# A convolution and expert kernel: the experts begin behind the first sort, and copies, first sums and the filter image are rearranged

## The chip, the core and the metric

The kernel runs on one core of a Trainium2 chip. The metric is the device time of one execution in microseconds (us); lower is better. Below, PE is the matrix engine (PEld its weight loads), DVE the vector engine, ACT the scalar engine, POOL the GpSimd engine and SP the engine that issues most of the DMAs. Each engine works through its own instructions in order.

## The reference

Eight sequences of 5696 rows of 128 columns are convolved with one filter along the rows. Each resulting row goes to one of eight two-layer expert networks, the one with the largest gate logit, and is scaled by its gate weight.

```python
L = 2 * S                                   # x: (8, 5696, 128), h: (5696, 128)
y = irfft(rfft(x, L, axis=1) * rfft(h, L, axis=0), L, axis=1)[:, :S]
x = y.reshape(B * S, D)                     # 45568 rows
logits = x @ w_gate                         # 8 experts
e = argmax(logits, axis=1)
gate_w = softmax(logits)[row, e]
out[row] = gate_w * (relu(x[row] @ w1[e]) @ w2[e])   # w1[e]: 128x1024, w2[e]: 1024x128
```

## The kernel before

The Fourier transforms are matrix products in two steps, and the eight sequences are worked on in three groups of 2, 3 and 3 (`SPLIT`). Names in the profile end in or contain the group's number in the order's rows (`pa1`, `xp1`, `mh1`), and the trace leaves the numbers out.

- **Transforms** (`phase_a`, `steps_a`): PE multiplies 120-row pieces of x (`xt`, split into `xc`) by a cosine and a sine matrix into `pa`; ACT and DVE copy the results (`ut`), and SP stores them in DRAM as `U`. The second and third group have 72 such steps each. The filter goes the same way once (`phase_h`, result `uht`).
- **Products** (`phase_b`), 120 items a group: SP loads `uq` from `U`; PE does the second step of the transform (`xp`); DVE multiplies by the filter's image `hh`, one product into `zt` and two halves into `xs` (L492, L495); POOL adds `zt` and `xs` (`combine`, L502: the first sums); PE transforms back (`vp`), and the result is copied to `vt` (`save`, L519: the result copies) and stored as `V`. The first group also makes the filter's image: PE multiplies (`hp`), ACT scales it into `hh` (L448), and SP stores it as `HS`, from which the two later groups load it.
- **Sort** (`phase_c`), 24 rounds of two steps (16 rounds in the first group): PE finishes the inverse transform (`yp`), ACT copies rows to `rt`, PE transposes and takes the logits (`tp`, `gb`), DVE finds each row's expert and place (`pi`), and POOL scatters the rows to the sorted table `SR` by indirect DMA (L581), 96 scatters in the first group and 144 in each later one. `pi` has 4 buffers. During the sort of the second group the transforms of the third are done as a guest. At the end `tables` (on DVE) lists the tiles of 256 rows.
- **Experts** (`moe`): for each tile SP loads rows `xr` from `SR` (7 buffers) and, when the expert changes, 2 MB of weights `wb` from `WD`; PE does layer 1 (`mh`, L985) and layer 2 (`ma`, L1005), ACT and DVE make the relu's two parts `hs` between them, DVE scales the result into `xr`, and POOL scatters it to `out` (L1028). Part 0, 1 and 2 of the tiles (37, 67 and 81) can begin when the first, second and third group is sorted. All scatters of a group must have landed before its first `xr` load.

The order of the instructions on every engine is fixed when the program is written: generators yield an estimated cost, and `run` takes the stream that is furthest behind, its cost divided by its share. `RATE` scales the costs of the background stream: entries 0, 1 and 2 are the second group's transforms, products and sort, 3, 4 and 5 the third group's. `LULL` is a pause of the expert stream behind the first sort, in which only the background stream runs, and its share there. After the third sort only experts are left.

```python
        run((first, 1.0), (prep, SHARES[1]), (back, SHARES[2]), until=first)
        run((prep, 1.0))
        lull = pause(LULL[0])
        run((lull, 1.0), (back, LULL[1]), until=lull)
        run((experts(), 1.0), (back, SHARES[3]))
```

Of the kernel before, what the change touches and what calls it, by code (L numbers as in the profile page):

```python
# [13 lines left out]
F32 = mybir.dt.float32  # L14
# [4 lines left out]
ALU = mybir.AluOpType  # L19
# [4 lines left out]
NB = 48  # L24
MB = 119
QN = 120
MP = 120
HP = 64
# [14 lines left out]
SAVEV = ()  # L43
# [5 lines left out]
GAPS = (0, 6000, 5000)  # L49
HOLD = (0, 0, 0)  # L50
AHEAD = 2
HEAD = 26000
A3 = (True, True, False)
ALO = ('gpsimd', 'vector', 'vector')
# [1 line left out]
WARM = 7  # L56
TURN = (1, 1, 1)
LOGIT = (2, 2, 2)
LULL = (29000, 0.448)
RARE = 3  # L60
XR = 7
RATE = (0.372, 0.559, 0.45, 0.8, 0.78, 0.6)


@with_exitstack
def conv_moe(ctx: ExitStack, tc: tile.TileContext, I, out, B, S, D, E, F, split):
    nc = tc.nc
# [67 lines left out]
    for g, nbs in enumerate(split):  # L135
# [7 lines left out]
            parts.append(gr.parts[-1])  # L143
            b0 += nb
        groups.append(gr)
    HS = dram.tile([P, QN, 2, D], F32, name="HS")
    WD = dram.tile([4, E * P, F], F32, name="WD")

    queue = []
# [158 lines left out]
    def phase_a(gr):  # L308
        start, begin, store, flush, M = steps_a(gr, "six", SIX)
        half = AT if gr.g == 0 else 750 * RATE[3 * gr.g - 3]  # L310
        start()
        for m in range(M + 2):
            if m < M:
                begin(m)
            yield half
            flush()
            if 1 <= m <= M:
                store(m - 1)
        yield 0
        flush()  # L320

    class Guest:
        def __init__(self, gr):
# [74 lines left out]
    def phase_b(gr):  # L398
# [15 lines left out]
        def load(qb):  # L414
            q = qb * QB
            if q >= QN:
                return
            uq = sb.tile([K2, QB, gr.cols], F32, tag="ld", name=f"uq{g}_{q}", bufs=LD if g else 3)
            nc.sync.dma_start(uq, gr.U[q : q + QB].rearrange("q p c -> p q c"))
            mi = mibufs[qb % 4]  # L420
            for k in range(2):
                nc.sync.dma_start(mi[k * HP : k * HP + NB], I["miq"][k * NB : (k + 1) * NB, q : q + QB, :])
            if g != 0:
                hhs[qb] = hhbufs[qb % 3]
                nc.sync.dma_start(hhs[qb][:, :QB], HS[:, q : q + QB])
            tiles[qb] = (uq, mi)

        mats, hhs, hbank, cuts = {}, {}, {}, {}
# [11 lines left out]
        def filt_save(qb, m):  # L440
            if qb not in hbank:
                return
            hp = hbank[qb]
            if m == 0:
                hhs[qb] = hhbufs[qb % 3]
            hh = hhs[qb]
            c2, k = divmod(m, 2)
            nc.scalar.mul(hh[k * HP : (k + 1) * HP, :, c2, :], hp[c2 * HP : (c2 + 1) * HP], -1.0 if m == 3 else 1.0)  # L448
            if m == 3:
                hbank.pop(qb)  # L450
                late.append((HS[:, qb * QB : qb * QB + QB], hh[:, :QB]))

        def forward(n):
            q, c = items[n]
# [44 lines left out]

        def combine(n):  # L500
            zt, xs = state[n]
            nc.gpsimd.tensor_tensor(out=zt, in0=zt, in1=xs, op=ALU.add)  # L502

        def inverse(n):
            q, c = items[n]
# [7 lines left out]
        def save(n):  # L513
            q, c = items[n]
            qb, k0 = divmod(q, QB)
            if k0 == 0 and c == 0:
                outs_[qb] = sb.tile([K2, QB, gr.cols], F32, tag="six", name=f"vt{g}_{q}", bufs=SIX)
            cp = nc.vector.tensor_copy if g == 0 or n % 4 in SAVEV else nc.scalar.copy
            cp(outs_[qb][:, k0, c * cw : (c + 1) * cw], banks.pop(n)[:K2, :cw])  # L519
            if k0 == QB - 1 and c == nch - 1:  # L520
                late.append((gr.V[qb * QB : qb * QB + QB].rearrange("q p c -> p q c"), outs_.pop(qb)))
                tiles.pop(qb), hhs.pop(qb), mats.pop(qb)
# [609 lines left out]
    def pause(ns):  # L1132
        yield ns
# [3 lines left out]
    def run(*streams, until=None, stop=()):  # L1137
        live = [[0.0, i, s, share] for i, (s, share) in enumerate(streams)]
        held = []
        while any(t[2] not in stop for t in live):  # L1140
            live.sort(key=lambda t: t[:2])
            it = live.pop(0)
            cost = next(it[2], DONE)
            if cost is None:
                held.append(it)
                continue
            now = it[0]
            if cost is DONE:
                if it[2] is until:
                    return  # L1150
            else:
                it[0] += cost / it[3]
                live.append(it)
            for t in held:
                t[0] = max(t[0], now)
            live += held
            held = []

    g0 = groups[0]
    with tc.manual_schedule():  # L1160
        prep = weights()
        back = rest()
        run((phase_a(g0), 1.0), (phase_h(), SHARES[4]), (consts(), 1.0), (prep, SHARES[5]), stop=(prep,))
        sb.close()
        sb.open("b")
        first = phase_b(g0)
        run((first, 1.0), (prep, SHARES[0]), until=first)
        sb.close()
        sb.close()
        sb.open("sb")  # L1170
        first = chain(*[gather(pt) for pt in g0.parts])
        run((first, 1.0), (prep, SHARES[1]), (back, SHARES[2]), until=first)
        run((prep, 1.0))
        lull = pause(LULL[0])
        run((lull, 1.0), (back, LULL[1]), until=lull)
        run((experts(), 1.0), (back, SHARES[3]))
        sb.close()
# [78 lines left out]
```

## Time and profile before

| | |
|---|---|
| time, median of 3 runs | 2405.68 us (2403.33 to 2406.07) |
| profiled execution: time, span | 2400.84 us, 2399.1 us |
| busy share of the span | PE 89%, DVE 67%, POOL 47%, ACT 44% |
| granted clock of PE, mean of the profiled execution | 0.951 of full speed |
| first group: products | about 117 to 340 us |
| first group: sort, with transforms of the second | about 366 to 495 us |
| first matmul of an expert | 570 us |
| first expert matmul of part 1 and end of the third sort on PE | 1190.5 us and about 1732 us |

The busy shares are means over stages with different limits. The stages' limits are read from the rows below: by stretch, a row of windows gives the busy time of every engine, PE's granted clock (1.00 is 2.4 GHz, 0.5 is 1.2 GHz) and the busy share of the DMA engines.

### The profile page before, as it was taken

How to read it: one execution, taken by the hardware profiler on the slowest of the kernel's cores; microseconds unless marked ns; L12 is line 12 of the kernel's file. 1: busy time of each engine (PE TensorE's matmuls, PEld its weight loads, DVE VectorE, ACT ScalarE, POOL GpSimd, SP SyncE). 2: the span in 40 equal slices, each digit the busy share in tenths (PEclk: the TensorE clock that was granted, in tenths of full speed). 3: DMA queues.
4: the chain of work that ended last, by engine and by line, in shares of the span. 5: the costliest groups of instructions: out<-in, count | busy, mean ns of one | idle time of the engine just before them, and what ended most of it. 6: DMA issues, size and time to landing. Idle time of an engine off the chain costs nothing.

```text
span 2399.1 us, 46517 instructions
## 1 busy us (share of the span) xinstructions
PE 2125.5 (89%) x13998; PEld 1759.0 (73%) x13998; DVE 1602.7 (67%) x3987; ACT 1049.3 (44%) x2233; POOL 1136.7 (47%) x1161
## 2 busy tenths in 40 slices
PE   7777759767999989998699998999979999999997
PEld 4654435444777777775377777988878999999997
DVE  3599965456999846667688885676654455555554
ACT  4533315432443445553144444665534444444443
POOL 5333323663555516677545553577762233333332
PEclk8899989878999999998799999999989999999998
DMA  9988879779999768877778775566322222222220
GB/s 268 294 256 266 271 205 321 234 214 265 271 269 276 213 191 248 258 234 218 220 202 252 210 236 148 124 167 175 95 87 85 76 74 81 75 79 75 80 75 30
DMA packets 226940, 444.88 MB, mean 185 GB/s; under 512 B 30993, under 2 KB 141639, under 8 KB 226688
## 3 DMA queue, kind: packets, MB, share of 16 engines
q1 hardware_dynamic: 202752, 394.78, 56.4%
q0 software_dynamic: 23936, 47.09, 6.5%
q8 instruction: 115, 1.88, 0.3%
q14 instruction: 137, 1.12, 0.2%
HBM read 597.98 MB, written 175.89 MB: 323 GB/s over the span
## 4 chain that ended last, share of the span: by engine, by line
PE 61%; DMA 12%; issue 6%; DVE 4%; POOL 2%; SPq 2%; ACT 1%; POOLq 0%; DVEq 0%; ACTq 0%
PE mh L985 18%; PE ma L1005 18%; PE vp L510 5%; PE xp L467 5%; DMA wb<-WD 5%; PE yp L644 5%; PE pa L279 3%; PE mx L167 2%; DMA SR<-rt,pi 2%; DMA xt<-x 2%; PE tp L683 1%; PE tp L167 1%; POOL out L1028 1%; DVE xs L495 1%; POOL SR L581 1%
## 5 line engine op out<-in xcount | busy, mean ns | idle before, releaser
L993 DVE SCALAR_TENSOR_TENSOR hs<-mh,hs 128x512 fp32r<-128x512 f32 x728 | 502.6, 691 | 473.4 <-ACT hs L991 467.6
L985 PE MATMUL mh<-xtb,wb 128*128 128x256 f32 x4368 | 728.8, 303 | 41.4 <-DMA wb<-WD 30.4
L985 PEld LDWEIGHTS mh<-xtb,wb 128*128 128x128 f32 x4368 | 596.6, 192 | 127.6 <-issue 66.2
L1028 POOL DMA_INDIRECT out<-xr x364 | 362.7, 996 | 681.1 <-DVE xr L1019 606.2
L1005 PE MATMUL ma<-hs,wb 128*128 128x256 f32 x4368 | 659.9, 287 | 10.4 <-DMA wb<-WD 10.2
L991 ACT ACTIVATE hs<-mh 128x512 fp32r<-128x512 f32 x728 | 435.3, 598 | 520.4 <-PE mh L985 518.3
L1005 PEld LDWEIGHTS ma<-hs,wb 128*128 128x128 f32 x4368 | 577.4, 192 | 14.4 <-DMA wb<-WD 13.9
L581 POOL DMA_INDIRECT SR<-rt,pi x384 | 397.3, 1035 | 208.5 <-issue 68.5
L502 POOL TENSOR_TENSOR zt<-zt,xs 128x384 f32<-128x384 f32 (+1 forms) x360 | 324.9, 916 | 313.2 <-DVE xs L495 303.5
L495 DVE TENSOR_TENSOR xs<-xp,hh 64x384 f32<-64x384 f32 (+1 forms) x720 | 367.8, 511 | 26.3 <-POOL zt L502 14.8
L467 PE MATMUL xp<-uq,mt 96*128 96x384 f32 (+1 forms) x720 | 284.1, 478 | 84.4 <-DVE xs L495 53.0
L510 PE MATMUL vp<-zt,mi 128*96 128x384 f32 (+1 forms) x720 | 269.9, 456 | 19.4 <-POOL zt L502 17.2
L519 ACT COPY vt<-vp 96x384 f32<-96x384 f32 x240 | 114.1, 475 | 358.3 <-PE vp L510 349.2
L467 PEld LDWEIGHTS xp<-uq,mt 96*128 96x128 f32 x720 | 118.8, 197 | 133.3 <-PE hp L438 60.9
L492 DVE TENSOR_TENSOR zt<-xp,hh 128x384 f32<-128x384 f32 (+1 forms) x360 | 183.3, 509 | 39.8 <-PE xp L467 19.5
L510 PEld LDWEIGHTS vp<-zt,mi 128*96 128x96 f32 x720 | 108.8, 164 | 113.4 <-issue 58.0
L279 PE MATMUL pa<-xc,fcr 120*120 120x512 f32 x360 | 110.6, 446 | 32.1 <-ACT xc L257 12.4
L448 ACT ACTIVATE hh<-hp 64x512 f32<-64x512 f32 x120 | 70.9, 591 | 142.4 <-issue 100.9
L644 PE MATMUL yp<-vr,gcr 120*120 120x384 f32 x576 | 117.0, 338 | 0.0
L632 DVE TENSOR_TENSOR vr<-vq,vr 120x768 fp32r<-120x768 f32 x96 | 91.5, 955 | 34.2 <-ACT vr L631 33.7
L279 PEld LDWEIGHTS pa<-xc,fcr 120*120 120x120 f32 x360 | 68.0, 203 | 59.0 <-ACT xc L257 17.2
L644 PEld LDWEIGHTS yp<-vr,gcr 120*120 120x120 f32 x576 | 96.2, 183 | 0.3 <-DVE vr L632 0.3
(121 smaller groups left out, 2028.3 us busy)
## 6 DMA issues: line engine op xcount, KB each, us to landing
wb<-WD SPq DMA_DIRECT2D x728, 512.0 KB
vq<-V SPq DMA_DIRECT2D x64, 720.0 KB
U<-ut SPq DMA_DIRECT2D x48, 720.0 KB
uq<-U SPq DMA_DIRECT2D x60, 576.0 KB
V<-vt SPq DMA_DIRECT2D x60, 576.0 KB
hh<-HS SPq DMA_DIRECT2D x60, 512.0 KB
xr<-SR SPq DMA_DIRECT2D x182, 130.0 KB
xt<-x SPq DMA_DIRECT2D x96, 240.0 KB
```

What stands on the lines that cost most here:

```text
L279: nc.tensor.matmul(banks[m][:QN, :], lhs, rhs, start=(k == 0), stop=(k == len(ops) - 1))
L467: nc.tensor.matmul(xp[:, :cw], mt[:, k0, :], uc, start=True, stop=True)
L495: nc.vector.tensor_tensor(out=xs[to], in0=x3[at], in1=hv[at, 1].broadcast_to([HP, cb, D]), op=ALU.mult)
L502: nc.gpsimd.tensor_tensor(out=zt, in0=zt, in1=xs, op=ALU.add)
L510: nc.tensor.matmul(vp[:K2, :cw], mi[:, k0, :], zt.rearrange("p b d -> p (b d)"), start=True, stop=True)
L581: s = nc.gpsimd.indirect_dma_start(out=SR[:, :], out_offset=IndirectOffsetOnAxis(ap=pi[:, b : b + 1], axis=0), in_=rt[:, b, :], in_offset= ...
L644: nc.tensor.matmul(yp[:MP, :cw], lhs, rhs, start=(m == 0), stop=(m == len(ops) - 1))
L985: nc.tensor.matmul(hp[:, u, :], wb[:, a, f, :], xt[:, b, :], start=(n == 0), stop=(n == 2))
L991: done = nc.scalar.activation(hs[:, 0], hp, AF.Relu)
L993: nc.vector.scalar_tensor_tensor(out=hs[:, 1], in0=hp, scalar=0.0, in1=hs[:, 0].bitcast(F32), op0=ALU.max, op1=ALU.subtract)
L1005: nc.tensor.matmul(accs[j], wb[:, a, f, :], hs[:, b, u, :], start=(k == 0 and u == 0 and n == 0), stop=(k == NPAIR - 1 and u == 1 and n == 2),
L1028: sc = nc.gpsimd.indirect_dma_start(out=out[:, :], out_offset=IndirectOffsetOnAxis(ap=xr[:, s, D + 1 : D + 2].bitcast(I32), axis=0), in_=x ...
```

## The change

Five things are edited. (1) All result copies go to ACT; before, those of the first group were on DVE. (2) `LULL` is shortened from 29000 to 12000, and from then on a step of the second group's transforms counts 1000 (`SLOW`) instead of 279, so that they are spread between the first expert tiles. (3) `RATE` gives the second group's products and sort lower costs (more of them per expert tile) and the third group's sort a higher cost (less of it per tile). (4) The first 20 sums of the third group are done by DVE (`ALONE`). (5) `HS` keeps 48 of every 64 partitions, in two DMAs instead of one for a store and for a load. No arithmetic is changed.

```diff
+ALONE = 20
-LULL = (29000, 0.448)
+LULL = (12000, 0.448)
+SLOW = 1000
-RATE = (0.372, 0.559, 0.45, 0.8, 0.78, 0.6)
+RATE = (0.372, 0.48, 0.42, 0.8, 0.78, 0.7)
...
-    HS = dram.tile([P, QN, 2, D], F32, name="HS")
+    HS = dram.tile([2, NB, QN, 2, D], F32, name="HS")
...
         for m in range(M + 2):
             if m < M:
                 begin(m)
-            yield half
+            yield half if not marks["experts"] else SLOW
             flush()
...
-                nc.sync.dma_start(hhs[qb][:, :QB], HS[:, q : q + QB])
+                for k in range(2):
+                    nc.sync.dma_start(hhs[qb][k * HP : k * HP + NB, :QB], HS[k, :, q : q + QB])
...
-                late.append((HS[:, qb * QB : qb * QB + QB], hh[:, :QB]))
+                for k2 in range(2):
+                    late.append((HS[k2, :, qb * QB : qb * QB + QB], hh[k2 * HP : k2 * HP + NB, :QB]))
...
-            nc.gpsimd.tensor_tensor(out=zt, in0=zt, in1=xs, op=ALU.add)
+            eng = nc.vector if g > 1 and n < ALONE else nc.gpsimd
+            eng.tensor_tensor(out=zt, in0=zt, in1=xs, op=ALU.add)
...
-            cp = nc.vector.tensor_copy if g == 0 or n % 4 in SAVEV else nc.scalar.copy
-            cp(outs_[qb][:, k0, c * cw : (c + 1) * cw], banks.pop(n)[:K2, :cw])
+            nc.scalar.copy(outs_[qb][:, k0, c * cw : (c + 1) * cw], banks.pop(n)[:K2, :cw])
...
         run((prep, 1.0))
+        marks["experts"] = True
         lull = pause(LULL[0])
```

**ACT in the first group's products.** Before, ACT makes only the filter's image there (`hh` from `hp`, four instructions a quarter of items) and casts weights (`wsp`):

```order
L448 ACTIVATE hh0_106<-hp0_15_1894 64x4x128 x4
L230 CAST wsp9_0_2019<-wraw9_1621 128x512
L448 ACTIVATE hh1_107<-hp0_16_1959 64x4x128 x4
L448 ACTIVATE hh2_108<-hp0_17_2024 64x4x128 x4
L448 ACTIVATE hh0_106<-hp0_18_2086 64x4x128 x2
```

In the changed program a result copy (`vt` from `vp`) stands between every two of them:

```order
L453 ACTIVATE hh1_107<-hp0_13_1778 64x4x128
L525 COPY vt0_44_1856<-vp0_44_0_1831 96x256
L453 ACTIVATE hh1_107<-hp0_13_1778 64x4x128
L525 COPY vt0_44_1856<-vp0_45_0_1848 96x256
L232 CAST wsp8_1_1871<-wraw8_1305 128x512
L453 ACTIVATE hh1_107<-hp0_13_1778 64x4x128
L525 COPY vt0_44_1856<-vp0_46_0_1862 96x256
```

The 120 copies left DVE's order, which there keeps `zt`, two `xs` and now and then a weight's second part.

**PE behind the first sort.** Before, all transforms of the second group (`pa1`) and the first nine items of its products (`xp1`, `vp1`) stand ahead of the first expert tile (`mx0`, `mh0`):

```order
L467 MATMUL xp1_6_0_5103<-uq1_4_5042,mt1_4_5040 128x384
L510 MATMUL vp1_2_0_5105<-zt1_2_0_5074,mi0_109 96x384
L467 MATMUL xp1_7_0_5119<-uq1_4_5042,mt1_4_5040 128x384
L510 MATMUL vp1_3_0_5121<-zt1_3_0_5084,mi0_109 96x384
L467 MATMUL xp1_8_0_5130<-uq1_8_5066,mt1_8_5049 128x384
L510 MATMUL vp1_4_0_5132<-zt1_4_0_5096,mi1_110 96x384
L167 MATMUL mx0_None_0_5191<-ident_87,xr0_0_5150 128x128 x2
L985 MATMUL mh0_0_0_5208<-xtb0_0_5194,wb0_0_5183 128x256 x6
```

Now six steps of `pa1` stand between the sort and the first tile, and the other 18 between its and the next tiles' matmuls:

```order
L281 MATMUL pa1_26_0_4914<-xc1_26_4895,fcr_84 120x512 x3
L281 MATMUL pa1_26_1_4919<-xc1_26_4895,fcr_84 120x512 x3
L169 MATMUL mx0_None_0_4973<-ident_87,xr0_0_4932 128x128 x2
L991 MATMUL mh0_0_0_4990<-xtb0_0_4976,wb0_0_4965 128x256 x6
L281 MATMUL pa1_27_0_5003<-xc1_27_4911,fcr_84 120x512 x3
L281 MATMUL pa1_27_1_5009<-xc1_27_4911,fcr_84 120x512 x3
L991 MATMUL mh0_0_1_5016<-xtb0_0_4976,wb0_0_4965 128x256 x6
L281 MATMUL pa1_28_0_5031<-xc1_28_5000,fcr_84 120x512 x3
L991 MATMUL mh0_0_2_5057<-xtb0_0_4976,wb0_1_4967 128x256 x6
```

The first `xp1` now stands behind 19 groups of `mh0`, 17 of `ma0` and all of `pa1`, in the fifth tile.

**POOL at the end of the second sort.** Before, the last two result scatters of part 0 stand inside the sort's last scatters, and the third group's sums follow:

```order
L1028 DMA out<-xr0_35_12129 45568x128 x2
L581 DMA SR_69<-rt1_20_12817,pi1_20_13366 366848x130 x5
L1028 DMA out<-xr0_36_12403 45568x128 x2
L581 DMA SR_69<-rt1_21_12987,pi1_21_13478 366848x130 x6
L581 DMA SR_69<-rt1_22_13164,pi1_22_13528 366848x130 x6
L581 DMA SR_69<-rt1_23_13329,pi1_23_13550 366848x130 x6
L502 TENSOR_TENSOR zt2_0_0_13681<-zt2_0_0_13681,xs2_0_0_13680 128x384
```

Now part 0's tiles end earlier in the sort, 37 scatters stand in a row behind the last of them, and the first sum on POOL is the 21st:

```order
L1034 DMA out<-xr0_36_12007 45568x128 x2
L587 DMA SR_69<-rt1_17_12577,pi1_17_13124 366848x130
L587 DMA SR_69<-rt1_18_12750,pi1_18_13251 366848x130 x6
L587 DMA SR_69<-rt1_19_12925,pi1_19_13362 366848x130 x6
L587 DMA SR_69<-rt1_20_13084,pi1_20_13464 366848x130 x6
L587 DMA SR_69<-rt1_21_13211,pi1_21_13541 366848x130 x6
L587 DMA SR_69<-rt1_22_13322,pi1_22_13588 366848x130 x6
L587 DMA SR_69<-rt1_23_13424,pi1_23_13605 366848x130 x6
L509 TENSOR_TENSOR zt2_20_0_14002<-zt2_20_0_14002,xs2_20_0_14001 128x384
```

The sort's last five steps (of `yp1`) and six steps of `pa2` moved behind part 0's last matmul on PE, and the sums 0 to 19 of the third group moved to DVE. Further on, an expert tile stands beside 7 items of the second group's products (6 before) and beside 1 round of the third sort (1.14 before), which therefore ends three tiles later, in tile 50 of part 1; what stands beside the third group's products is as before.

## Rows read from the trace of the kernel before

**Rows 1.** Windows: stretch, length, busy us (instructions) of each engine, granted clock, DMA share, GB/s.

```profile
140.00:335.00 195.00, 138.86 (x613) 95.94 (x612) 184.14 (x427) 66.40 (x112) 75.28 (x105) 0.98 0.84 262
360.00:420.00 60.00, 54.89 (x300) 34.02 (x300) 33.22 (x148) 33.41 (x81) 21.11 (x21) 0.95 0.98 322
495.00:570.00 75.00, 38.37 (x107) 22.37 (x107) 38.59 (x103) 16.31 (x30) 35.84 (x34) 0.73 0.83 240
570.00:828.00 258.00, 256.34 (x1386) 190.14 (x1387) 238.56 (x439) 102.12 (x217) 142.18 (x144) 0.99 0.91 260
...
1121.00:1190.00 69.00, 36.28 (x92) 15.32 (x90) 47.85 (x132) 9.31 (x21) 45.62 (x46) 0.74 0.81 226
1487.00:1726.00 239.00, 236.20 (x1949) 216.61 (x1948) 165.36 (x613) 144.35 (x344) 162.96 (x155) 0.98 0.57 141
1726.00:1779.00 53.00, 34.57 (x251) 33.24 (x250) 29.41 (x106) 14.59 (x32) 40.66 (x41) 0.80 0.34 98
```

**Rows 2.** Groups of instructions, DVE, 140 to 335 us: count | busy us, mean ns | idle before.

```profile
L495 DVE TENSOR_TENSOR xs<-xp,hh 64x256 f32<-64x256 f32 x208 | 87.8, 422 | 4.4
...
L519 DVE COPY vt<-vp 96x256 f32<-96x256 f32 x104 | 43.8, 421 | 3.3
L231 DVE TENSOR_TENSOR wsp<-wraw,wsp 128x512 fp32r<-128x512 f32 x10 | 9.3, 933 | 0.3
```

**Rows 3.** Groups of instructions by shape, ACT, whole run.

```profile
L519 ACT COPY vt<-vp 96x384 f32<-96x384 f32 x240 | 114.1, 475 | 358.3 <-PE vp L510 349.2 <-DMA mt<-mq 3.6 <-DMA hh<-HS 2.7
...
L1015 ACT COPY ot<-ma 128x256 f32<-128x256 f32 x182 | 68.0, 374 | 20.3 <-PE ma L1005 4.4
```

**Rows 4.** DMA issues, 140 to 335 us: the filter image's stores.

```profile
HS<-hh SPq DMA_DIRECT2D x26, 512.0 KB
```

**Rows 5.** Timeline around the first tile: start, length, engine, line; idle time before in brackets.

```profile
529.63 1.02 POOL L581 DMA_INDIRECT SR<-rt,pi  x1 [0.30 <-issue]
...
549.16 4.82 PE L467 MATMUL xp<-uq,mt 96*128 96x384 f32 x8 [12.60 <-DMA uq<-U]
...
561.83 2.65 SPq L935 DMA_DIRECT2D xr<-SR  x3
...
570.23 1.62 PE L985 MATMUL mh<-xtb,wb 128*128 128x256 f32 x6 [1.33 <-DMA wb<-WD]
```

**Rows 6.** The chain of waits, 470 to 640 us: start, length, what.

```profile
584.37 0.71 PE mh L985 x6
...
585.79 0.65 PE xp L467 x2
```

**Rows 7.** The same chain: two neighbouring steps of the first sort.

```profile
482.29 1.29 PE yp L644 x4
...
485.33 1.29 PE yp L644 x4
```

**Rows 8.** Timeline of PE behind part 0's last tile.

```profile
1125.48 5.09 PE L467 MATMUL xp<-uq,mt 96*128 96x384 f32 x8 [1.94 <-issue]
...
1154.23 1.59 PE L510 MATMUL vp<-zt,mi 128*96 128x384 f32 x2 [16.19 <-POOL zt L502]
...
1190.53 1.62 PE L985 MATMUL mh<-xtb,wb 128*128 128x256 f32 x6 [1.50 <-DMA wb<-WD]
```

**Rows 9.** Groups, DVE: a split in 495 to 535 us; the later groups' halves, whole run.

```profile
L258 DVE TENSOR_TENSOR xc<-xt,xc 120x512 fp32r<-120x512 f32 x11 | 7.6, 691 | 13.2 <-ACT xc L257 13.2
...
L495 DVE TENSOR_TENSOR xs<-xp,hh 64x384 f32<-64x384 f32 x480 | 266.5, 555 | 21.3 <-POOL zt L502 14.8
```

**Rows 10.** Groups, POOL, 1535 to 1726 us; then its timeline around the third sort's last scatter.

```profile
L581 POOL DMA_INDIRECT SR<-rt,pi x108 | 113.6, 1051 | 32.9 <-issue 11.0 <-DMA SR<-rt,pi 4.3 <-ACT rt L659 4.3
...
1771.43 0.99 POOL L581 DMA_INDIRECT SR<-rt,pi  x1 [0.30 <-issue]
```

**Rows 11.** Timeline of DVE and PE behind the third sort.

```profile
1738.44 0.21 DVE L776 TENSOR_REDUCE pi<-rk 120x6 int32<-120x54 f32 x1 [3.87 <-DMA SR<-rt,pi]
...
1778.49 1.62 PE L985 MATMUL mh<-xtb,wb 128*128 128x256 f32 x6 [6.78 <-DMA wb<-WD]
```

More of the change, by code (lines that the diff above doesn't have):

```diff
@@ L320, in phase_a @@
         flush()
+    marks = {"experts": False}
     class Guest:
```

## The prediction

> **What bounds the kernel now.** I read the windows first, stretch by stretch, because the page's busy shares are means over stages with different limits, and then, in each stretch that the change touches, the groups and waits of the engine that is nearest to full.
>
> In the first group's products DVE is busy 184.14 of 195 us, 94%; PE, POOL and ACT are far below and the DMA engines at 0.84 [rows 1]. 105 items pass in it [rows 2], so an item takes 195/105 = 1.857 us. Between the sort and the first expert tile, 495 to 570 us, nothing is full: PE is busy half of the time, at 0.73 of its clock [rows 1]. The second group's products beside experts are PE's (256.34 of 258 us), with DVE at 92% behind it [rows 1]. From 1121 to 1190 us PE is idle for half again: the third group's products run there without expert work [rows 1]. In the third sort PE is full (236.20 of 239 us [rows 1]), but from about 1535 us POOL's queue has no gap: 108 scatters show 113.6 us busy and 32.9 idle, which is 1.36 us apiece with 0.30 between them, the bare issue; its last sort scatter starts at 1771.43 us, some 40 us behind PE's end of the sort [rows 10]. Behind it DVE waits 3.87 us for a scatter and PE 6.78 us at the next new weights [rows 11], and 1726 to 1779 us has 0.80 of the clock [rows 1].
>
> **The change part by part,** against the profiled execution's 2400.84 us, 0.2% under the median of 2405.68.
>
> *Copies to ACT, smaller filter image: -38 us.* An item costs DVE two halves, one product and a copy; the 104 copies take 43.8 us and 3.3 idle [rows 2]. Without them DVE's floor is (195 - 47)/105 = 1.41 us an item. PE's is 138.86/105 = 1.32. ACT has 66.40/105 = 0.63 and receives a copy; a 96x256 copy on ACT is in no row, so I bound it by 0.374 (128x256) and 0.475 us (96x384) [rows 3], which gives at most 1.11. POOL has 0.72. So the DMA engines come next: 0.84 x 1.857 = 1.56 us an item. `HS` stores were 26 of 512 KB [rows 4], 13.6 of the 51.1 MB (262 GB/s x 195 us [rows 1]); a quarter less is 6.5%, leaving 1.46 at a share of 1.00. The highest share that a stretch keeps is 0.98, the usual busy one 0.91 [rows 1]; I take 0.95, since the stores are many and large, so 1.54 us. The saving is (1.857 - 1.54) x 120 items = 38 us. Bounds: 48 us at a share of 1.00, 53 if DVE's floor decides, 19 if the share stays near 0.86 (1.70 us).
>
> *Experts between the last transforms: +6 us.* The first tile stands in PE's order 18 transform steps and nine items earlier, but its `xr` waits until all 96 scatters have landed. POOL issues the last at 529.63 us; I put its landing at 533. From the load's issue to the first `mh` it was 570.23 - 561.83 = 8.4 us [rows 5]. So the first `mh` stands at about 542, not 520: 28 us earlier than before, and PE runs dry ahead of it, since only six transform steps are left there. Then come 19 groups of `mh`, 17 of `ma` and 18 of `pa1`, at 0.71 us each [rows 6] 38 us, with two tiles' transposes 41, and some 3 for the clock that the idle time cost: 586 us. Then the last `U` must be stored and loaded: `xp1` waited 12.60 us for that before [rows 5], of which 2 to 3 are now covered. The first `xp1` is at 596 us. Before, the same 36 groups (26 us) and transposes begin at 570.2 us with nine `xp1` and five `vp1` already done (14 x 0.65 = 9 us [rows 6]): it stands at the same state at 590. The loss is 6 us. Bounds: -4, if the store is quick, and +25, if the early weight loads hold up the `U` stores on SP's queue and PE waits the whole 12.60 and more.
>
> *Seven items a tile instead of six: +2 us.* Total work is unchanged. In 258 us the 120 items, less nine, were 18.5 tiles of 13.9 us, 12.9 of them DVE's; one more item adds 1.3 to PE (two `xp` or `vp` groups [rows 6]) and 3 x 0.555 = 1.7 to DVE [rows 9], so DVE goes from 0.92 to 14.6/15.2 = 0.96 of PE's time. PE still sets the pace; I allow 2 for waits (0 to 5). The smaller `HS` loads are hidden here by PE.
>
> *Second to third group: -3 us.* Part 0 now ends ahead of the second sort's last five steps. A step takes 485.33 - 482.29 = 3.04 us [rows 7], so these are 15 us that now stand between part 0's last `ma` and `xp2`; storing and loading the last `U` is taken as 5 more. `xp2` comes 20 us later against that `ma`. But the time ahead of it loses that PE work: a step with a transform beside it has 54.89/60 x 3.04 = 2.8 us of PE [rows 1], times five 14 us. POOL has 37 scatters behind part 0, at 1.3 us 48 us; before, `vp` waited 16.19 us for a sum behind them [rows 8]. The 20 first items now don't ask POOL: each costs DVE 3 x 0.555 and a sum, which I size as 0.691 x 384/512 = 0.52 [rows 9], 2.2 us in all; 20 of them 44 us, and POOL is free by then. With 12 us of lead and tail the products ahead of the first `mh` take 56 us instead of 1190.53 - 1125.48 = 65 [rows 8]: -9. The sum is 20 - 14 - 9 = -3. Bounds: -12 if the sort steps fill PE's idle half, +20 if DVE's sums are held up.
>
> *Third sort: -13 us.* Beside a tile POOL had 6 x 1.14 + 2 = 8.9 instructions and now has 8, at 1.36 us 10.9 instead of 12.1; 34 result scatters, 17 tiles, took 191 us, 11.2 a tile. So POOL's lag stops growing, and only 14 scatters instead of 17 stand behind the last tile's results; the waits of 3.87 and 6.78 us [rows 11] go, and about 3 of the 53 x 0.20 = 11 us of clock. Bounds: 0, if the lag is only moved, and -22.
>
> The sum is -38 + 6 + 2 - 3 - 13 = -46, or 2355 us on the profiled scale and 2360 on that of the medians.
>
> **The rivals.** *R1, the DMA engines give less than I take.* The image's two half stores may take as long as the whole did. Then 1.56 us of transfers stay, at a share of 0.92 a step of 1.70 us, and 19 us are saved: total -27, 2379 us. For it: 0.84 was seen with DVE, not the transfers, at its limit [rows 1]; against it: 0.98 was kept for 60 us. Chance 0.13. The Trainium skill speaks against edit 5: "SBUF — State Buffer", section "Door 1: The DMA port swizzle", holds that a transfer of partitions 0 to 63 reaches half of the ports, 196 GB/s at 1 MiB against 328 for 128 partitions, and the section on two DMAs that two halves run one behind the other. By that the image's 0.41 us an item would become 0.75 x 328/196 x 0.41 = 0.52 and the step about 1.67/0.95 = 1.75 us, a saving of 12; no row of before shows a 48-partition store by itself.
>
> *R2, the early tiles cost the second group more.* Weight loads of 512 KB enter SP's queue ahead of the last `U` stores; at the upper bound, +25, the total is -27, 2379 us. For it: a wait of 12.60 us stood there with SP nearly empty [rows 5]. Chance 0.09.
>
> *R3, DVE's sums and POOL's scatters block each other.* Each of 20 sums would wait out up to one scatter (1.02 us [rows 5]), and the third group's start moves by 20: +20 instead of -3, total -23, 2383 us. A split with two inputs in SBUF took 933 ns in the first products, where POOL sums run [rows 2], and 691 ns while POOL scatters [rows 9], so scatters seem not to hold it. Chance 0.06. The Trainium skill, "SBUF — State Buffer", section "Who interferes with whom", has such a DVE instruction contend with a GpSimd instruction that reads SBUF, and the later one wait in full; the two rows agree only if a scatter's issue doesn't count as such a read.
>
> *R4, the other side: ACT's order becomes the loop.* A copy waits for `vp`, hence for POOL's sum; `hh` stands behind the copy on ACT, and an `hh` that waits for an old `HS` store now holds up copies, PSUM and PE. At 2.0 us an item the first products lose 17 us instead of gaining 38: total +9, 2415 us. It decides from 1.92 us an item on, where the 8 that the rest saves are spent, which asks for 0.8 us of waiting on ACT's 1.1 of work. Against it: ACT is idle two thirds of the time, and quarters are separate buffers. Chance 0.07.
>
> *R5, DVE's floor is reached.* The transfers keep nearly 1.00, and 53 us are saved: 2345 us. Chance 0.05.
>
> **How the numbers follow.** The forecast has 0.60, at 2348 to 2372 by the middle of its terms' bounds. The range from 2338 to 2392 takes in R1, R2, R3 and R5 and the bounds of each term singly, and leaves out R4 and several bad terms together. A measurement of this kernel tells 0.2%, about 5 us, from no change. R4, and R1 to R3 in combination, end slower with 0.06 or within 0.2% with 0.05; the other 0.89 are faster.
>
> **What would show it.** In the first products: no copies on DVE, DVE near 0.9 or less, the DMA share at 0.95, an item near 1.54 us, ACT's copy near 0.4 us. Behind the first sort: `mh` about 28 us earlier against POOL's last scatter, idle PE ahead of it with the cause `xr` from `SR`, and a wait of `xp1` for `U` in the fifth tile. Between second and third group: DVE sums near 0.52 us, no `vp` waiting for POOL. At the third sort's end: POOL's lag under 30 us, no 3.87 and no 6.78. It is wrong if the first products' share stays below 0.9 with DVE idle, or if the wait for `U` behind the early tiles exceeds 20 us.

## The result, and the profile after

The changed kernel takes 2375.11 us (median of 4 runs, 2370.04 to 2384.09) against 2405.88 us: a ratio of 0.9876 (95% interval 0.9842 to 0.991). It is faster, as forecast, by 31 us where the forecast said 46. The execution whose profile is read here is the longest of the four: 2384.09 us, 9 above its median, with a span of 2382.3 us; before's profile lies 5 below its median. So between the two profiles the change is worth only 16.8 us, and where terms are compared below, they are compared between these two.

The windows of the changed kernel (stretch, length, busy us of PE, PEld, DVE, ACT and POOL, granted clock, DMA share, GB/s):

```profile
117.00:283.00 166.00, 151.05 (x691) 100.09 (x690) 156.92 (x364) 113.47 (x241) 88.98 (x117) 0.99 1.01 317
...
440.00:491.00 51.00, 16.39 (x66) 9.77 (x63) 20.57 (x96) 8.72 (x20) 32.49 (x32) 0.58 0.47 129
491.00:545.00 54.00, 42.64 (x288) 39.19 (x288) 26.32 (x44) 23.08 (x44) 7.80 (x8) 0.91 0.75 241
600.00:817.00 217.00, 210.94 (x1085) 152.09 (x1083) 198.46 (x364) 80.96 (x177) 118.98 (x121) 0.98 0.96 248
1062.00:1101.00 39.00, 29.53 (x188) 18.60 (x186) 24.69 (x140) 17.57 (x46) 27.02 (x26) 0.94 0.62 172
1102.00:1183.00 81.00, 58.23 (x82) 21.59 (x80) 56.24 (x122) 8.81 (x19) 23.86 (x25) 0.52 0.66 166
1489.00:1736.00 247.00, 244.68 (x2037) 225.86 (x2038) 171.09 (x614) 146.77 (x352) 168.78 (x160) 1.00 0.58 147
1736.00:1790.00 54.00, 41.10 (x331) 39.05 (x330) 35.00 (x127) 19.67 (x44) 41.25 (x42) 0.93 0.22 61
```

The first row answers to the first of [rows 1]: all 120 items of the first products now pass in 166.7 us (first `xp` at 116.63, last at 283.34), 1.40 us an item instead of 1.86. DVE is as full as before (156.92 of 166 us, 0.945), without the copies, and not at 0.9 or less as the forecast had it. The groups of DVE, and then of ACT, from 140 to 260 us (count | busy us, mean ns | idle before), which answer to [rows 2, 3]:

```profile
L501 DVE TENSOR_TENSOR xs<-xp,hh 64x256 f32<-64x256 f32 x169 | 71.3, 422 | 3.6
L498 DVE TENSOR_TENSOR zt<-xp,hh 128x256 f32<-128x256 f32 x85 | 36.1, 425 | 2.7
L233 DVE TENSOR_TENSOR wsp<-wraw,wsp 128x512 fp32r<-128x512 f32 x9 | 6.2, 693 | 0.3
```

```profile
L453 ACT ACTIVATE hh<-hp 64x512 f32<-64x512 f32 x85 | 50.2, 591 | 1.6
L525 ACT COPY vt<-vp 96x256 f32<-96x256 f32 x85 | 31.2, 368 | 34.4 <-PE vp L517 30.5 <-DMA uq<-U 3.8
```

A copy costs ACT 368 ns, and ACT is still idle 36 of 120 us.

Behind the first sort, PE's timeline (start, length, line, idle time before and its releaser):

```profile
486.27 0.69 PE L169 MATMUL mx_None<-ident,xr 128*128 128x128 f32 x2 [19.00 <-DMA xr<-SR]
491.40 1.62 PE L991 MATMUL mh<-xtb,wb 128*128 128x256 f32 x6 [4.44 <-DMA wb<-WD]
...
545.23 1.62 PE L473 MATMUL xp<-uq,mt 96*128 96x384 f32 x2 [9.90 <-DMA uq<-U]
```

POOL's last scatter of that sort starts at 481.57 us. The first `mh` comes 9.8 us behind it and the first `xp1` 63.7; the forecast had 12 and 66. PE runs dry for 19.00 us ahead of the first tile with the cause it named, and waits 9.90 us for `U` behind the early ones.

Between the second and the third group things went otherwise than forecast. PE there:

```profile
1101.47 5.39 PE L473 MATMUL xp<-uq,mt 96*128 96x384 f32 x8 [4.03 <-DMA uq<-U]
1116.94 1.62 PE L473 MATMUL xp<-uq,mt 96*128 96x384 f32 x2 [10.08 <-DVE xs L501]
...
1141.96 1.65 PE L473 MATMUL xp<-uq,mt 96*128 96x384 f32 x2 [0.56 <-ACT vt L525]
1143.40 1.49 PE L517 MATMUL vp<-zt,mi 128*96 128x384 f32 x2
1145.45 1.65 PE L473 MATMUL xp<-uq,mt 96*128 96x384 f32 x2 [0.56 <-ACT vt L525]
...
1183.10 1.62 PE L991 MATMUL mh<-xtb,wb 128*128 128x256 f32 x6 [2.81 <-DMA wb<-WD]
```

No `vp` waits for POOL any more, but an item takes 1145.45 - 1141.96 = 3.49 us. Each `xp` waits 0.56 us for ACT's copy of the `vp` ahead of it, PE has a gap in every item, and the granted clock is 0.52 over the whole 81 us. From 1120 to 1180 us it is 0.50, the lower of PE's two levels, without a break:

```profile
1120.00:1140.00 20.00, 16.97 (x25) 6.23 (x24) 17.05 (x31) 2.85 (x6) 8.78 (x9) 0.50 0.62 147
1140.00:1160.00 20.00, 16.62 (x24) 6.05 (x23) 13.35 (x24) 2.84 (x6) 0.00 (x0) 0.50 0.44 104
1160.00:1180.00 20.00, 17.14 (x26) 6.38 (x24) 11.13 (x20) 2.37 (x5) 1.26 (x1) 0.50 0.61 146
```

The one run without gaps in this stretch, the eight matmuls from 1101.47 us, took the clock to 1.00 from 1108 to 1110 us; PE was waiting then (10.08 us), and by 1112 it was down again. Before, the same items ran without such gaps once POOL was free, and an item took 1.5 to 1.75 us. PE's clock rose behind the first of them and stayed up to 1180 us:

```profile
1154.00:1160.00 6.00, 5.76 (x12) 2.59 (x12) 5.55 (x10) 1.42 (x3) 5.00 (x6) 0.72 0.40 120
1160.00:1165.00 5.00, 4.97 (x15) 2.15 (x15) 4.83 (x9) 1.42 (x3) 2.83 (x3) 1.00 0.53 127
...
1170.00:1180.00 10.00, 9.35 (x25) 3.57 (x24) 9.66 (x18) 3.29 (x7) 5.62 (x7) 1.00 1.06 309
```

From the first `xp2` to the first `mh` of part 1 it is now 81.6 us instead of 65.0 [rows 8].

At the end of the third sort, DVE, POOL and PE, answering to [rows 10, 11]:

```profile
1748.74 0.21 DVE L782 TENSOR_REDUCE pi<-rk 120x6 int32<-120x54 f32 x1 [0.42 <-DVE rt L760]
```

```profile
1782.32 1.00 POOL L587 DMA_INDIRECT SR<-rt,pi  x1 [0.30 <-issue]
```

```profile
1789.38 1.62 PE L991 MATMUL mh<-xtb,wb 128*128 128x256 f32 x6 [3.57 <-DMA wb<-WD]
```

The wait of 3.87 us is 0.42, that of 6.78 is 3.57, and the clock behind the sort is 0.93 instead of 0.80.

Where the time went is best read at marks with the same work behind them in both kernels. The last scatter of the first sort: 48.1 us earlier than before. The first `mh` of part 1 (all of part 0, the second sort and the third group's first 20 items lie behind it): 7.4 earlier. The last `xp2`: 3.5. The end: 16.8. So 48 us were won ahead of the first expert tile, 41 lost again up to the third group's first 20 items, 4 more beside its other items, and 13 won behind them.

### The profile page after: what moved, and what is told of

The parts are those of the page before. It is cut to its first block, busy times and chain, and to the rows that moved or that the text cites. A ratio compares the mean times of both kernels' runs of the same rounds, so it can differ in the third digit from the quotient of the medians.

```text
span 2382.3 us, 46587 instructions
## 1 busy us (share of the span) xinstructions
PE 2147.2 (90%) x13998; PEld 1758.3 (74%) x13998; DVE 1565.7 (66%) x3887; ACT 1087.4 (46%) x2353; POOL 1118.3 (47%) x1141
## 4 chain that ended last, share of the span: by engine, by line
PE 69%; DMA 12%; issue 8%; DVE 5%; POOL 3%; SPq 1%; ACT 1%; POOLq 0%; DVEq 0%; ACTq 0%
PE mh L991 18%; PE ma L1011 18%; PE vp L517 8%; PE xp L473 8%; DMA wb<-WD 6%; PE yp L650 5%; PE pa L281 5%; DMA SR<-rt,pi 3%; PE mx L169 3%; DVE xs L501 2%; PE tp L689 2%; PE tp L169 1%; POOL SR L587 1%; POOL out L1034 1%; DMA HS<-hh 1%
## 5 line engine op out<-in xcount | busy, mean ns | idle before, releaser
L509 POOL TENSOR_TENSOR zt<-zt,xs 128x384 f32<-128x384 f32 (+1 forms) x340 | 310.4, 927 | 275.7 <-DVE xs L501 184.5
L525 ACT COPY vt<-vp 96x384 f32<-96x384 f32 (+1 forms) x360 | 158.2, 439 | 424.6 <-PE vp L517 409.5
L517 PE MATMUL vp<-zt,mi 128*96 128x384 f32 (+1 forms) x720 | 285.0, 479 | 17.4 <-DVE xs L501 6.8
L638 DVE TENSOR_TENSOR vr<-vq,vr 120x768 fp32r<-120x768 f32 x96 | 91.6, 956 | 48.6 <-ACT vr L637 48.1
L293 ACT COPY ut<-pa 120x512 f32<-120x512 f32 x96 | 56.3, 587 | 88.7 <-PE pa L281 80.2
```

The source lines that it names most:

```text
L509: eng.tensor_tensor(out=zt, in0=zt, in1=xs, op=ALU.add)
L517: nc.tensor.matmul(vp[:K2, :cw], mi[:, k0, :], zt.rearrange("p b d -> p (b d)"), start=True, stop=True)
```

## The experiments

The theory after this profile had three parts. A1: the 53 us of the first products come from DVE's copies alone. A2: 20 sums on DVE lead, by the order in which PSUM banks come free, to gaps on PE and so to half clock. A3: an early start of the experts uses up tiles that are then missing between second and third group. The rivals: the low clock was an accident of one execution; the first products' gain is partly given back whatever else is done; the smaller filter image did part of the work.

Four kernels run together share a chip and the runs of the kernel before. That kernel took 2540 us beside e1 to e4, 2401 beside e5 to e8 and 2555 beside e9 to e12, so times are compared only among kernels that ran together. On the two slower chips the stretch behind the third group's products is 66 to 100 us longer, with either cost of the third sort.

**The changed kernel again.**

> The changed kernel once more, for a second profile. In the first, the stretch from the first product of the third group (xp2) to the first expert tile of part 1 took 81.6 us instead of 65, with PE at half clock throughout and 3.49 us an item. Theory A (the program causes it: PE never gets a run without gaps, because each xp waits for the copy of a vp): 0.50 to 0.55 of the clock and 78 to 84 us again; time 2370 to 2384. Theory B (an accident of that execution): 0.7 or more, 60 to 68 us, and a profiled time near 2365.

Measured: 2511 us against 2540, ratio 0.9879 (0.9841 to 0.9916). Its window of that stretch:

```profile
1161.00:1243.00 82.00, 59.04 (x84) 21.69 (x84) 58.26 (x137) 8.80 (x19) 23.88 (x24) 0.53 0.64 161
```

82 us at 0.53 again, on a chip where the kernel before takes 2540 us: the program causes it, and the accident is out. The absolute times expected don't apply on this chip.

**No sums on DVE.**

```diff
-ALONE = 20
+ALONE = 0
```

> All first sums of the third group on POOL again (ALONE 0), all else as changed. Theory A (half clock from the bank order, started by the early small pieces): POOL's sums come only behind the 37 scatters, some 29 us after the first xp2, and then 20 items pass at 1.7 us with full clock, 65 to 70 us: 10 to 15 us faster than the changed kernel, about 2362. Theory C (the sums on DVE do what was forecast and the loss is elsewhere): the wait for the scatters is back, 10 to 20 us slower, about 2390.

Measured: 2490 us, ratio 0.9799 (0.9764 to 0.9834), 22 us faster than e1. The first `vp` waits for POOL's sum again:

```profile
1178.03 1.59 PE L517 MATMUL vp<-zt,mi 128*96 128x384 f32 x2 [14.64 <-POOL zt L509]
```

Then an item takes 1.5 us, with the clock at 0.98 from 1184 to 1200 us; from the first `xp2` to the first `mh` it is 68 us, 14 less than in e1, as theory A said. The other 8 of the 22 us lie outside the stretch and are not explained. Theory C is out. Edit 4 loses.

**Banks of their own.**

```diff
-            xp = ps.tile([P, 512], F32, tag="cx", name=f"xp{g}_{q}_{c}", bufs=4)
+            xp = ps.tile([P, 512], F32, tag="c0", name=f"xp{g}_{q}_{c}", bufs=2)
...
-            vp = ps.tile([P, 512], F32, tag="cx", name=f"vp{g}_{q}_{c}", bufs=4)
+            vp = ps.tile([P, 512], F32, tag="c1", name=f"vp{g}_{q}_{c}", bufs=2)
```

The other users of the four banks (`pa`, `yp`, `tp`, `gb`) take `c0` and `c1` in turn.

> The changed kernel with xp and vp in PSUM banks of their own (two each; the others alternate between the same two pairs), so that an xp waits for the product of the second last xp and never for a copy of a vp. Order on all engines is unchanged. Theory A: PE's gaps of 0.56 us in the handover go, the clock rises, 20 items take 2.3 to 2.6 us, the stretch 55 to 65 us: 15 to 25 us faster, about 2355. Theory D (DVE's 2.3 us an item alone keep PE too idle for full clock): the clock stays near 0.5, an item at 2.6 to 2.9 us, 10 us faster or less.

Measured: 2505 us, ratio 0.9849 (0.9807 to 0.9891), 6 us faster than e1. The window, and PE in it:

```profile
1161.00:1228.00 67.00, 40.76 (x85) 16.60 (x85) 58.37 (x137) 8.81 (x19) 25.50 (x25) 0.73 0.77 199
```

```profile
1195.12 1.62 PE L481 MATMUL xp<-uq,mt 96*128 96x384 f32 x2 [0.45 <-DVE xs L509]
1196.53 1.49 PE L525 MATMUL vp<-zt,mi 128*96 128x384 f32 x2
1197.81 1.49 PE L481 MATMUL xp<-uq,mt 96*128 96x384 f32 x2
1199.09 1.49 PE L525 MATMUL vp<-zt,mi 128*96 128x384 f32 x2
1200.37 1.10 PE L481 MATMUL xp<-uq,mt 96*128 96x384 f32 x2
1201.31 0.81 PE L525 MATMUL vp<-zt,mi 128*96 128x384 f32 x2
...
1204.42 0.88 PE L481 MATMUL xp<-uq,mt 96*128 96x384 f32 x2 [0.79 <-DVE xs L509]
1205.14 0.81 PE L525 MATMUL vp<-zt,mi 128*96 128x384 f32 x2
1206.75 0.88 PE L481 MATMUL xp<-uq,mt 96*128 96x384 f32 x2 [0.79 <-DVE xs L509]
```

With the same order of instructions, an `xp` now waits for DVE and not for a copy. Between 1195 and 1201 us PE gets a run without gaps and then the higher clock, and from there an item takes 2.33 us, DVE's pace. The stretch is 15 us shorter. So the bank order is what kept PE at half clock. The gap by itself does not do it: once the clock is up, it stays at 1.00 from 1205 to 1222 us, though PE then waits 0.79 us in every 2.33:

```profile
1205.00:1222.00 17.00, 11.42 (x31) 4.55 (x29) 16.28 (x30) 3.32 (x7) 0.00 (x0) 1.00 0.90 226
```

Theory A's 15 us came in the stretch (67 us, just above its 55 to 65), but only 6 of them are left in the whole. The second sort lost by the change: from the last `xp1` to the first `xp2` e3 takes 340 us and e1 330.

**Copies and image alone,** on the kernel before (edits 1 and 5).

```diff
-            cp = nc.vector.tensor_copy if g == 0 or n % 4 in SAVEV else nc.scalar.copy
-            cp(outs_[qb][:, k0, c * cw : (c + 1) * cw], banks.pop(n)[:K2, :cw])
+            nc.scalar.copy(outs_[qb][:, k0, c * cw : (c + 1) * cw], banks.pop(n)[:K2, :cw])
```

with the image's three edits as in the change.

> The kernel before with the copies on ACT and the filter image in two halves alone. The forecast sized this at -38 us; the profile shows the products 52 us shorter. Theory A (the 52 reach the end, and the other edits lost 20 of them): 50 us faster than before, about 2355. Theory E (a part is given back in later stages whatever else is changed): 30 to 40 us faster, 2366 to 2376, and the other edits cost or gain little.

Measured: 2496 us, ratio 0.9825 (0.9791 to 0.9858): 44 us faster than before and 15 faster than e1. Between the two expectations: edits 2 to 4 together cost 15 us here.

**Eight sums and own banks.** `ALONE = 8` in e3's kernel.

> The changed kernel with banks of their own for xp and vp, and only the first 8 sums of the third group on DVE. Theory A (half clock came from the bank order, and 20 sums on DVE are more than the scatters' tail asks for): 8 items at 2.3 us cover the scatters, the other 12 pass at 1.5 to 1.7 us, so the stretch from xp2 to the first mh of part 1 takes about 60 us instead of 67 (banks alone) and 68 (no sums on DVE); against its kernel before a ratio of 0.975 to 0.979. Theory C (any sum on DVE loses against POOL): 66 us or more, ratio 0.980 to 0.985.

Measured: 2372 us, ratio 0.9883 (0.9856 to 0.991). The stretch is 60.8 us, as Theory A said, and the ratio is that of the changed kernel: theory A's total was wrong. Shortening this stretch did not repair what its neighbours lose: the last group of `mh` of part 0 and the first of part 1 are still 103 us apart, against 74 before, and from the last `xp1` to the first `xp2` it takes 300 us, against 285 in e8 with the four banks in turn.

**Copies alone,** the image whole: the diff of e4 without the image.

> The kernel before with the copies on ACT alone, the filter image whole. Theory A (the transfers decide behind DVE, and the image's rows count): 1.56 us of transfers an item at a share near 1.00, so the first products take about 187 us instead of 167 with the smaller image and 220 before. Theory F (the halved image saves nothing, as two half transfers take as long as one whole): 165 to 170 us as with the halves, and the same time as the kernel with both edits.

Measured: 2349 us, ratio 0.9783 (0.9758 to 0.9809), 52 us faster than before. The first products take 166.7 us, to the tenth what they take with the halves; theory A, that the transfers decide, is refuted. This kernel's window from 140 to 260 us, and then that of the changed kernel:

```profile
140.00:260.00 120.00, 109.96 (x510) 72.02 (x508) 113.54 (x264) 83.68 (x178) 65.37 (x85) 1.00 1.04 347
```

```profile
140.00:260.00 120.00, 109.99 (x511) 72.16 (x510) 113.49 (x263) 84.02 (x179) 65.52 (x85) 1.00 1.02 324
```

The smaller image takes 7% of the bytes away and changes nothing else. The equal times alone would also fit theory F, in which the halves cost the transfers as much as the whole; DVE's order decides. In these 120 us no instruction of DVE waits in either kernel: its 6.5 us of idle lie in 262 pieces of less than 0.06 us. So DVE sets the pace in both.

**Copies, image and costs** (edits 1, 3 and 5): e4's kernel with the new `RATE`.

> Edits 1, 3 and 5 on the kernel before: copies, costs of the background stream, image. By the forecast's terms the costs are worth -13 us in the third sort and +2 in the second products, so 11 us faster than edits 1 and 5 alone (2496 in the last comparison). By the profile after, the second products lost 10 instead of 2: 3 us faster. If the costs gain nothing on this chip, whose third sort is slower, the same time as edits 1 and 5; what the kernel without DVE sums has beyond this run is the early experts' (edit 2).

Measured: 2329 us, ratio 0.9692 (0.9668 to 0.9716): 72 us faster than before, 20 faster than copies alone, more than the 11 expected, and with the lowest ratio of all kernels here (all edits: 0.9876). By the last `xp2` e6 and e7 are level, so the 20 us lie behind it, in the third sort and the experts after it, as e8 shows next. Without the early start, seven items a tile leave tiles of part 0 over for the time between second and third group: the longest time from one group of `mh` to the next is 33 us instead of 74.

**No sums on DVE, third sort as before.**

```diff
-RATE = (0.372, 0.48, 0.42, 0.8, 0.78, 0.7)
+RATE = (0.372, 0.48, 0.42, 0.8, 0.78, 0.6)
```

> The changed kernel without DVE sums and with the third sort's cost at its old 0.6 (1.14 rounds beside a tile instead of 1). The forecast's step: POOL's queue grows again, its last sort scatter comes 10 us or more later behind PE's end of the sort, and the kernel is 13 us slower than without DVE sums alone (2490 in the last comparison), 2503. Rival: the lag is only moved, the time is within 5 us.

Measured: 2377 us, ratio 0.9895 (0.987 to 0.9921). Against e7 it has edit 2 and the third sort's old cost, and is 48 us slower. POOL's last sort scatter comes 54 us behind PE's last `yp`, 48 in e7: 6 later, not 10 or more. Read at the marks: its last `xp2` is at 1434.1 us, e7's at 1404.0, so edit 2 loses 30 us by there; from there to the end of the span it takes 942.4 us, e7 923.9, so the third sort's cost is worth 18. The same stretch is 940.9 before and 944.2 in e6 (old cost), 927.6 in the changed kernel and 924.3 in e5 (new cost): 13 to 20 in each pair. The stretch with the third group's first items in e8, and in e7:

```profile
1097.00:1165.00 68.00, 35.90 (x85) 15.67 (x86) 45.17 (x102) 8.81 (x19) 44.26 (x44) 0.75 0.77 201
```

```profile
1085.00:1160.00 75.00, 67.16 (x329) 45.38 (x328) 63.71 (x116) 24.67 (x51) 44.38 (x45) 0.95 0.86 230
```

The first PE column is the reading: 36 of 68 us without expert tiles, 67 of 75 with them, at a clock of 0.75 and 0.95.

**All edits but the sums, again; and the same with cover.** The second of these keeps the early start and lets fewer tiles stand beside the second group:

```diff
-RATE = (0.372, 0.48, 0.42, 0.8, 0.78, 0.7)
+RATE = (0.372, 0.42, 0.32, 0.8, 0.78, 0.7)
```

> All edits but the sums on DVE (ALONE 0), now beside the next three on one chip. Theory A (edit 2 fills PE's wait behind the first sort with tiles that are missing between second and third group, so it gains nothing there and costs the cover): the third sort's new cost is worth 13 to 19 us against the same kernel with the old one (2377), so 2358 to 2364, which is 29 to 35 slower than edits 1, 3 and 5 without edit 2 (2329). Theory G (edit 2 is neutral, and the difference was the third sort's cost alone): within 10 us of 2329.

> As e9, but the second group's products cost 0.42 (0.48) and its sort 0.32 (0.42), so that fewer expert tiles stand beside them: in the order, tile 35 of part 0 is the last ahead of the third group's first product, as in the kernel without edit 2, and 36 beside its first 20 items. Theory A (what is missing is cover): PE stays busy between the groups, 25 to 35 us faster than e9, 2325 to 2340. Theory H (early experts cost by their own stage: DVE full, clock, late U): 10 us or less faster than e9, 2350 or more.

Measured: 2508 us (ratio 0.9819, 0.979 to 0.9848) and 2506 us (0.9812, 0.9785 to 0.9839). The stretch with the third group's first items, without and with cover:

```profile
1159.00:1227.00 68.00, 35.70 (x85) 15.29 (x85) 46.83 (x116) 8.81 (x19) 43.68 (x45) 0.75 0.75 194
```

```profile
1161.00:1240.00 79.00, 72.36 (x350) 49.29 (x349) 68.28 (x125) 26.66 (x55) 38.47 (x39) 0.94 0.85 227
```

Cover does there what A3 says: the longest time from one group of `mh` to the next falls from 114 to 32 us, and the last `xp2` comes at 1477.2 instead of 1496.0 us, 19 us earlier and 2 behind e11's 1475.7, which has no early start. But the median gains only 2 us: from that mark to the end e10 took 1025 us, e9 1014. So the mechanism is shown up to the end of the third group's products; for the whole, on this chip, the expectation of 25 to 35 failed, theory H's 10 or less is what came, and why its third sort is longer stays open.

**Copies and costs,** the image whole: e7's kernel without edit 5.

> Edits 1 and 3 with the filter image whole. Theory A (DVE's floor decides in the first products with either image, and later PE covers the loads): the same time as with the halves (2329) within 5 us. Theory F2 (fewer bytes help the second group, where the transfers are at 0.97): 8 us or more slower.

Measured: 2499 us, ratio 0.9787 (0.9757 to 0.9816), 9 us faster than e9, and 20 by the last `xp2`. They differ by edit 2 and by the image. Edit 2 seems to lose here too, but by the medians not the 29 to 35 us that were expected of e9: 9 us lies inside theory G's 10. e7 itself did not run on this chip, so what the image is worth in the later groups is not settled; in the first products e6 shows that it is nothing.

**Own banks without the other two edits:** e7's kernel with e3's banks.

> Edits 1, 3 and 5 with banks of their own for xp and vp. If an xp's wait for a copy costs beside experts too (products of the second and third group), 5 to 10 us faster than 2329, about 2321. If it costs only where PE has nothing else, the same time within 4 us.

Measured: 2522 us, ratio 0.9883 (0.9852 to 0.9914), 24 us slower than e11, from which it differs by the banks and the image's halves. Its last `xp1` is 12 us later and its last step of the second sort 23 later. Neither expectation was right. From the last `xp1` to the first `xp2` it takes 382 us, e11 372. With e3 and e5 that makes three pairs in which own banks cost 10 to 15 us in the second sort, where the third group's transforms share the same banks; in the third sort, without that guest, e3 and e12 lose 1 and 2. That fixed pairs leave these steps fewer free banks is the likely reason, and it was not tried apart.

Another 7 us of e12's loss lie in the second products (270.8 us from first to last `xp1` against 263.9), and there the image is the suspect: e7, with the halves and the four banks in turn, takes 271.0. With six items a tile e4 (halves) takes 284.2, e6 and the kernel before (whole) 279.1 and 279.4. One and the same code gave 267.7 to 272.9 there in five executions on several chips, so this is a sign that the halves cost something in the later groups, and not a proof.

## Why the prediction was right, and where it was off

*The sign and the main mover* were right: DVE bound the first products, and taking 120 copies from it was the gain.

*The first products* were sized at 38 us and gave 53. The step that failed is "the DMA engines come next", with 1.46 us an item at a share of 1.00 and 1.54 at the 0.95 that was taken. The changed kernel needed 1.40, at a share of 1.02, and with the whole image, for which the forecast's reckoning gives 1.56, e6 needed the same 1.40 at 1.04. So the share did not stop at 0.95, and it was read as if it grew in proportion to the bytes: 262 GB/s at 0.84 would be 312 at 1.00, but e6 moved 347 at 1.04. What decided was DVE's own floor, the rival R5, to which the forecast gave 0.05. R1's step of 1.70 us is refuted. Its premise is not: with the halves the bytes fell by 7% and the share only from 1.04 to 1.02, which DVE's pace hides. The rule of the Trainium skill cited there ("SBUF — State Buffer", "Door 1: The DMA port swizzle") shows nothing in the time: by the forecast's estimate from its figures the step would have been 1.75 us, and halves and whole both measured 1.40.

*Experts behind the first sort*, +6: as a local step it was right. `xp1` came 63.7 us behind the last scatter, the forecast had 66.4. With before's same state taken from the forecast (590, 60 behind its last scatter) the loss is 3. But the step asked only when things start. It did not ask where the four tiles that now run early are missing.

*Second to third group*, -3: this is the step that failed. By its own pieces: from the last `mh` of part 0 (1062.12) to the first `xp2` it is 39.4 us, before 9.0 (from 1116.49), so 30 later instead of 20; from there to the first `mh` of part 1 81.6 instead of the forecast's 56. With the forecast's own 14 us for the PE work that moved there, the term is 30 + 17 - 14 = +33. Two mechanisms stand behind it. One is the bank order with half clock: own banks took 15 us of the stretch away in e3, and no sums on DVE 14 in e2. The forecast took DVE's pace of 2.2 us for the item's; e3 shows that pace (2.33), but it holds only where PE is not at half clock; the changed kernel took 3.49. The other is that expert tiles are the cover for such stretches: part 0 has 37 of them, and each that runs early runs out early. e7 against e8 shows it with the sums on POOL in both (30 us by the last `xp2`), e10 against e9 by putting the cover back (19).

*R3* forecast a loss of that kind at this place, by another mechanism, and that one is out. A sum on DVE, while POOL's scatters still ran (until 1130 us):

```profile
1118.60 0.56 DVE L509 TENSOR_TENSOR zt<-zt,xs 128x384 f32<-128x384 f32 x1
1119.19 0.56 DVE L498 TENSOR_TENSOR zt<-xp,hh 128x384 f32<-128x384 f32 x1
```

It takes 0.56 us, the forecast's 0.52, with no wait. The rule of the Trainium skill on two inputs ("SBUF — State Buffer", "Who interferes with whom") does not bite against scatters here. And the split that took 933 ns beside POOL's sums in [rows 2] takes 693 in the changed kernel, also beside sums, so that row was no clean witness for it. R2's wait for `U` stayed at 9.90 us, and R4's loop did not form: ACT is idle 36 of 120 us in the first products.

*Seven items a tile*, +2: what remains of the 41 us lost between the marks is about 5, if the two terms above are taken at 3 and 33. Ahead of these marks another 5 of the 53 us went in the first sort. It was not measured by itself: e6 and e7, with six and seven, have their last `xp2` at the same time, but there the seven also bought cover.

*The third sort*, -13: measured 13.3 from the last `xp2` to the end, and 13 to 20 in the other pairs on such chips. From that mark on PE is idle 53.2 us instead of 61.5, and its busy time is 5 us less. Of the waits named in it one went as said (3.87 us to 0.42) and the other halved (6.78 to 3.57). One of its signs was wrong: POOL's last scatter comes 35 us behind PE's end of the sort (its last `gb`), before 40, not "under 30". On the slower chips the gain is not seen: 1010 us with the old cost in e4, 1007 to 1025 with the new one.

The result lay in the range because two misses had opposite signs: 15 us more won in the first products, and some 36 more lost between second and third group. That is luck: the mechanism of the largest loss was not in the forecast. In which stage the other executions save the 9 us by which the profiled one lies above the median is not shown.

## What to carry to other kernels

Work that covers another stage's waits is a stock: when a change uses it earlier, ask which later stretch it covered, and count the longest time in which the covered engine has nothing else. When an engine is relieved, size the next limit by its own instructions' durations; the DMA share of a stretch in which the transfers had time to spare is no measure of what they can do. When work moves to another engine, look at which release the next PE instruction then waits for. In these kernels PE's clock rose behind a run without gaps and then outlasted short ones; a wait in every item from the first on left no such run, and that took back what moving the sums was to bring.

## What the runs showed of the hardware that was not expected

The DMA share went to 1.04 at 347 GB/s in e6, above one, while 0.84 had gone with 262. PE stayed at 0.50 of its clock from 1120 to 1180 us although it was busy 51 of these 60 us, with a gap of 0.56 us in every 3.49; in e3 it stayed at 1.00 from 1205 to 1222 us though busy only 11.4 of these 17. And the same kernel before took 2401, 2540 and 2555 us on three chips, and 2406 in the first comparison. In the third sort of e1, on one of the slower chips, PE waited up to 3.5 us for ACT's `rt`, and ACT waited 36.8 us in all, up to 6.9 at a time, for something that the trace puts on no instruction of the core; the changed kernel's first profile has neither. Each chip ran once, so what makes this was not found.
